# Two loads of 40 partitions cut into four, of 32 and of 8 partitions, in a kernel of mLSTM attention and two feed-forward layers

## Chip, cores, metric

One Trainium2 chip, one core. The metric is device time in microseconds of one launch, over several runs; smaller is better.

## What is computed

Three layers, one after the other, in float32.

1. An mLSTM attention over q, k, v of shape (2, 8, 768, 40): two batches, eight heads, 768 steps, 40 wide. For every step t and head:

```
m_new = max(f + m, i);  fs = exp(f + m - m_new);  is = exp(i - m_new)
C = fs * C + is * outer(v_t, k_t);   n = fs * n + is * k_t
y_t = sigmoid(o_t) * (C q_t) / max(|n . q_t|, 1)
```

2. A mixture of eight experts over the 1536 tokens (320 wide, 1024 inner). Noisy logits choose the best two experts of a token, softmax weights them, each expert is `relu(x w1) w2`.

3. A dense layer: `h = x w_in` (2048 wide), `g = h cos(h)`, result `g w_out`.

## The kernel before

**Attention.** The 768 steps of a batch are cut into NC = 6 pieces of 128 steps, so that there are 12 attention steps (`att_step(n)`, L858, n from 0 to 11, six for each batch). Within a piece the recurrence becomes matmuls: `mm_s` (L240) forms k times q for four pairs of heads, `mk_w` (L200) forms the decay weights by exponentials, `mk_p` (L251) multiplies both, `mm_out` (L300) multiplies by v and adds the part of the running state, `mm_state` and `mk_state` (L261, L281) carry the state on, `mk_q` (L233) scales q for the next piece, and `mk_y` (L316) divides and gates and stores the result `xt` in the DRAM tensor `xd`. All instructions are issued in an order written by hand: step n does the matmul `mm_s` for piece n+2, and its own `mm_out`, interleaved per pair of heads (L869 to L877).

**Loads.** All plain transfers are issued by SyncE (SP) in program order. `load_qk(n)` (L162) brings q and k of a piece into one of NB = 3 tiles `qk` of 128 partitions by 4 x 4 x 128 values. Even heads lie in partitions 0 to 39 and odd heads in 64 to 103; the other partitions stay zero from the start (L137, L138). A half is 40 rows of 3 x 4 x 128 values of 4 bytes, 6144 bytes each, contiguous in DRAM. `load_gb` (L171) reads the cumulated forget gates from the DRAM tensor `gd`, where `gates_a` (L85) has written them, and spreads them over all partitions; `load_kv` (L179) brings k and v by rows, `load_o` (L153) the output gates. `loads(n+1)` (L847) at the end of step n issues q and k of piece n+4, then `gb`, `kv` and, in the first steps, `ogt`. The tile `qk` that is filled again is the one that the multiplication of L238 (`qtt`, on POOL or DVE) has read for piece n+1. The store of `xt` (L330) follows on the same queue. Three pieces of q and k are loaded ahead of the first step (L817 to L822).

**Experts.** From step 6 on the router of batch 0 (`router_*`) runs between the steps, and weights of the first expert are loaded (`load_w`, L533, tile `wraw`). From step 9 on, expert steps (`expert_step`, L640) stand among the attention steps; each splits its weights into two float32r parts (L589, L591) and does three products in place of one (`mm1`, L594; `mm2`, L600). The dense layer follows in the same manner. This part, from about 95 us to the end, is most of the time.

Of the kernel before, what the change touches and what calls it, by code (L numbers as in the profile page):

```python
# [19 lines left out]
B, H, S, D = 2, 8, 768, 40  # L20
# [21 lines left out]
def tile_mlstm_moe_moe2(ctx, tc, qk, kv, og, gi, gf, wcat, noise, wm1, wm2, cst, out):  # L42
    nc = tc.nc
    V, A, G, T, Y = nc.vector, nc.scalar, nc.gpsimd, nc.tensor, nc.sync
# [89 lines left out]
    for i in range(NB):  # L134
        t = ap_.tile([128, 4, NH, C], FT, name=f"qk{i}")
# [4 lines left out]
    for i in range(2):  # L140
        t = ap_.tile([128, H, 64], FT, name=f"kb{i}")
        G.memset(t, 0.0)
        KBS.append(t)
    for i in range(2):
        t = ap_.tile([128, NH, 82], FT, name=f"st{i}")
# [16 lines left out]
    def load_qk(n):  # L162
        if n >= 2 * NC:
            return
        b, c = divmod(n, NC)
        d = L[n]
        t = d["qk"] = QKS[n % NB]
        Y.dma_start(t[0:D, 0:3], qk[b, c, 0])
        Y.dma_start(t[64:64 + D, 1:4], qk[b, c, 1])

    def load_gb(n):  # L171
        if n >= 2 * NC:
# [642 lines left out]

    Y.dma_start(ident, cst[:, 0:128])
    load_qk(0)  # L817
    load_kv(0)
    load_qk(1)
    load_o(0)  # L820
    load_kv(1)
    load_qk(2)  # L822
    gates_a(0, 1)
    gates_b(0, 1)
# [193 lines left out]
    for q in range(3):  # L1018
        for i in range(3):
            c = 3 * q + 3 + i  # L1020
# [25 lines left out]
    with tc.If(over > 0):  # L1046
        WD = [dr.tile([S, E], FT, name=f"wd{b}") for b in range(B)]
        for b in range(B):
            r = R[b]
# [6 lines left out]
        for b in range(B):  # L1056
            with tc.For_i(0, NC, 1) as it:
# [11 lines left out]
                for e in range(E):  # L1069
                    acc = psA()  # L1070
                    for f in range(8):
# [3 lines left out]
                        for k in range(3):  # L1075
                            r = slice(64 * (k == 2), 128)
# [20 lines left out]
                t = mp.tile([128, DM], FT, name="yt", tag="yt", bufs=3)  # L1097
# [76 lines left out]
```

## Time and profile before

| | us |
|---|---|
| median of three runs | 521.35 |
| the three runs | 517.87, 521.35, 522.74 |
| the profiled execution's own time | 519.47 |
| its span, first to last instruction | 517.8 |

The profiled execution's own time is its span and 1.67 us around it. Times in views are counted from the start of the span. PE is TensorE's matmul, PEld its weight load, DVE is VectorE, ACT ScalarE, POOL GpSimd, and a "q" behind an engine's name its queue.

### The profile page before, as it was taken

The page shows a single profiled execution, that of the slowest core. Times are in us where ns is not written, and L with a number is a line of the kernel's source. Part 1 is how long each engine was busy: PE and PEld are TensorE (multiplying, and loading weights), DVE is VectorE, ACT ScalarE, POOL GpSimd, SP SyncE. Part 2 cuts the span into 40 slices and gives each one's busy share as a digit, 9 for nine tenths or more (in the row PEclk, how much of TensorE's full clock was granted, in tenths as well). Part 3 has the DMA queues.
Part 4 walks back from the last instruction along what each step waited for, and adds up shares of the span by engine and source line. Part 5 has one row for each costly group of instructions (what it writes and reads, how often), then busy time and mean ns, then how long its engine had stood idle before and what let it go on. Part 6 is the DMA issues. An engine that isn't in the chain of part 4 may idle for free.

```text
span 517.8 us, 9017 instructions
## 1 busy us (share of the span) xinstructions
PE 489.4 (95%) x3198; PEld 469.2 (91%) x3198; DVE 368.6 (71%) x787; ACT 326.1 (63%) x695; POOL 274.6 (53%) x234
## 2 busy tenths in 40 slices
PE   4899989999999999999999997899999999999995
PEld 3798978899899999999999997899999999999994
DVE  8885595678468776778775678788855655787772
ACT  3658864566555554545454575578877777777772
POOL 6435456666856867595868686274355347300000
PEclk9999997999999999999999999999999999999999
DMA  6878883595472928290929193130021003001001
GB/s 182 252 264 276 271 276 120 174 331 204 172 287 87 338 67 319 85 379 22 367 92 315 58 362 118 42 104 14 1 70 47 1 1 103 13 2 38 2 1 44
DMA packets 25397, 76.37 MB, mean 147 GB/s; under 512 B 3872, under 2 KB 11392, under 8 KB 25344
## 3 DMA queue, kind: packets, MB, share of 16 engines
q1 hardware_dynamic: 22752, 67.11, 37.3%
q0 software_dynamic: 2592, 8.61, 5.4%
q8 instruction: 27, 0.44, 0.3%
q14 instruction: 26, 0.21, 0.1%
HBM read 66.47 MB, written 9.22 MB: 146 GB/s over the span
## 4 chain that ended last, share of the span: by engine, by line
PE 74%; DVE 12%; DMA 5%; ACT 5%; issue 3%; POOL 1%; SPq 0%; DVEq 0%; POOLq 0%; ACTq 0%
PE pS L598 35%; PE pA L607 11%; PE pA L604 10%; PE pA L603 10%; PE pM L559 2%; PE pA L616 1%; PE pA L615 1%; DMA gb<-gd 1%; DMA qk<-qk 1%; ACT wt L210 1%; DMA wraw<-wm 1%; PE pS L311 1%; DVE c_t L721 1%; DVE ogt L325 1%; DVE r_am L489 1%
## 5 line engine op out<-in xcount | busy, mean ns | idle before, releaser
L591 POOL TENSOR_TENSOR wl<-wraw,wh 128x704 fp32r<-128x704 f32 x69 | 122.9, 1790 | 61.0 <-ACT wh L589 53.5
L653 DVE SCALAR_TENSOR_TENSOR hb<-pS,hb 128x384 fp32r<-128x384 f32 (+2 forms) x128 | 45.9, 390 | 45.5 <-ACT hb L650 44.8
L589 ACT ACTIVATE wh<-wraw 128x704 fp32r<-128x704 f32 x80 | 62.9, 786 | 14.0 <-PE pA L615 9.1
L598 PE MATMUL pS<-xh,wh 128*128 128x448 f32 (+1 forms) x240 | 69.7, 344 | 0.7 <-ACT xh L561 0.5
L598 PE MATMUL pS<-xh,w 128*128 128x384 f32 x288 | 66.5, 340 | 1.6 <-DVE m_t L762 1.5
L598 PE MATMUL pS<-xh,wl 128*128 128x448 f32 (+1 forms) x240 | 65.7, 328 | 0.4 <-POOL wl L591 0.4
L604 PE MATMUL pA<-wl,hb 128*128 128x320 f32 x208 | 62.2, 308 | 0.0
L603 PE MATMUL pA<-wh,hb 128*128 128x320 f32 x208 | 62.0, 307 | 0.0
L747 ACT ACTIVATE m_t<-pS,magic 128x384 f32<-128x384 f32 x64 | 37.1, 580 | 27.9 <-PE pS L598 27.1
L650 ACT ACTIVATE hb<-pS 128x448 fp32r<-128x448 f32 (+1 forms) x80 | 37.7, 472 | 26.3 <-PE pS L598 19.3
L598 PEld LDWEIGHTS pS<-xh,w 128*128 128x128 f32 x288 | 49.8, 188 | 2.9 <-DVE m_t L762 2.9
L762 DVE SCALAR_TENSOR_TENSOR m_t<-m_t,pS 128x384 f32<-128x384 f32 x64 | 35.4, 553 | 16.8 <-ACT m_t L761 16.2
L607 PE MATMUL pA<-wh,hb 128*128 128x320 f32 x208 | 44.0, 310 | 2.8 <-DVE hb L653 2.7
L598 PEld LDWEIGHTS pS<-xh,wl 128*128 128x128 f32 x240 | 42.7, 188 | 2.9 <-POOL wl L591 0.5
L598 PEld LDWEIGHTS pS<-xh,wh 128*128 128x128 f32 x240 | 40.4, 189 | 2.0 <-ACT xh L561 0.6
L748 DVE TENSOR_SCALAR m_t<-m_t 128x384 f32<-128x384 f32 x64 | 23.1, 361 | 26.6 <-ACT m_t L747 26.4
L768 POOL TENSOR_TENSOR wl<-m_t,wh 128x384 fp32r<-128x384 f32 x25 | 25.5, 1018 | 30.3 <-ACT wh L766 21.2
L598 PE MATMUL pS<-xl,wh 128*128 128x448 f32 (+1 forms) x160 | 39.6, 328 | 0.1
L603 PEld LDWEIGHTS pA<-wh,hb 128*128 128x128 f32 x208 | 38.6, 186 | 0.8
L604 PEld LDWEIGHTS pA<-wl,hb 128*128 128x128 f32 x208 | 38.6, 186 | 0.6
L550 POOL DMA_INDIRECT xgt<-xd,idx x28 | 34.4, 1229 | 7.0 <-issue 2.5
L749 DVE SCALAR_TENSOR_TENSOR m_t<-pS,m_t 128x384 f32<-128x384 f32 x64 | 35.7, 558 | 2.2
(196 smaller groups left out, 1243.7 us busy)
## 6 DMA issues: line engine op xcount, KB each, us to landing
wraw<-wm SPq DMA_DIRECT2D x36, 704.0 KB
raw<-wm SPq DMA_DIRECT2D x16, 704.0 KB
qk<-qk SPq DMA_DIRECT2D x24, 240.0 KB
gb<-gd SPq DMA_DIRECT2D x10, 512.0 KB
kv<-kv SPq DMA_DIRECT2D x12, 324.0 KB
yd<-yt SPq DMA_DIRECT2D x22, 160.0 KB
wraw<-wm SPq DMA_DIRECT2D x8, 352.0 KB
ogt<-og SPq DMA_DIRECT2D x6, 320.0 KB
```

The source lines that it names most:

```text
L550: G.indirect_dma_start(out=t[:n, :], out_offset=None, in_=XD[0:S, :] if g < 2 else XD[:, :], in_offset=bass.IndirectOffsetOnAxis(ap=(idxe ...
L589: A.activation(wh, raw[:, f, :], AF.Copy)
L591: eng.tensor_tensor(out=wl, in0=raw[:, f, :], in1=wh.bitcast(FT), op=OP.subtract)
L598: T.matmul(p[:, :n], w[:, 128 * k:128 * k + 128], x[:, m, :], start=(i == 0), stop=(i == 7))
L603: T.matmul(a[:n, :DM], hh[:, s], wh[:, KW:], start=first, stop=False)
L604: T.matmul(a[:n, :DM], hh[:, s], wl[:, KW:], start=False, stop=False)
L607: T.matmul(a[:n, :DM], hl[:, s], wh[:, KW:], start=False, stop=last)
L650: A.activation(hh[:, :n], p[:, :n], AF.Relu)
L653: V.scalar_tensor_tensor(out=hb[:, o:o + z - a], in0=p[:, a:z], scalar=0.0, in1=hh[:, a:z].bitcast(FT), op0=OP.max, op1=OP.subtract)
L747: A.activation(t, m["p"], AF.Identity, bias=magic, scale=0.5 / PI)
L749: V.scalar_tensor_tensor(out=t, in0=m["p"], scalar=0.5 / PI, in1=t, op0=OP.mult, op1=OP.subtract)
L762: V.scalar_tensor_tensor(out=s, in0=s, scalar=1.0, in1=m["p"], op0=OP.subtract, op1=OP.mult)
```

## The change

The two loads of a `load_qk`, each of 40 partitions, become four: first partitions 0 to 31 of the even half, then of the odd half, then the remaining 8 partitions of each. Bytes, tiles, and the place in the program stay.

```
-        Y.dma_start(t[0:D, 0:3], qk[b, c, 0])
-        Y.dma_start(t[64:64 + D, 1:4], qk[b, c, 1])
+        for r in (slice(0, 32), slice(32, D)):
+            for s in range(2):
+                Y.dma_start(t[64 * s + r.start:64 * s + r.stop, s:s + 3], qk[b, c, s, r])
```

## Rows read from the trace of the kernel before

**Rows 1.** The page's span, and DMA's mean share in 40 equal slices.
```profile
span 517.8 us, 9017 instructions
...
DMA  6878883595472928290929193130021003001001
```
**Rows 2.** The page's chain that ended last: share of the span by engine, by line.
```profile
PE 74%; DVE 12%; DMA 5%; ACT 5%; issue 3%; POOL 1%; SPq 0%; DVEq 0%; POOLq 0%; ACTq 0%
PE pS L598 35%; PE pA L607 11%; PE pA L604 10%; PE pA L603 10%; PE pM L559 2%; PE pA L616 1%; PE pA L615 1%; DMA gb<-gd 1%; DMA qk<-qk 1%; ACT wt L210 1%; DMA wraw<-wm 1%; PE pS L311 1%; DVE c_t L721 1%; DVE ogt L325 1%; DVE r_am L489 1%
```
**Rows 3.** Attention stage: stretch, length, busy per engine (count), clock share, DMA share, GB/s.
```profile
16.00:76.00 60.00, 55.21 (x426) 51.07 (x424) 43.12 (x130) 42.58 (x127) 30.73 (x44) 1.00 0.88 279
```
**Rows 4.** Waits, 16 to 76 us: who for whom, us in total, times, longest.
```profile
ACT wt L210 <- DMA gb<-gd: 1.2, 1, 1.2
...
PE pA L248 <- DMA qk<-qk: 1.0, 2, 0.8
```
**Rows 5.** The chain in order of time, 27 to 49 us: start, us, what.
```profile
27.78 1.23 DVE g_all L97 x2
...
29.02 2.45 DMA gd<-g_all
...
31.54 6.00 DMA gb<-gd
...
37.62 1.29 ACT wt L210 x4
...
41.93 1.28 POOL qtt L238
...
43.59 5.95 DMA qk<-qk
```
**Rows 6.** Timeline of PE at three waits: start, us, ..., [idle before <-releaser].
```profile
23.56 0.45 PE L248 MATMUL pA<-qk 128*128 128x256 f32 x1 [0.81 <-DMA qk<-qk]
...
42.42 0.38 PE L356 MATMUL pM<-wc,xTt 128*128 128x128 f32 x1 [1.03 <-ACT xTt L349]
...
49.66 0.46 PE L248 MATMUL pA<-qk 128*128 128x256 f32 x1 [0.19 <-DMA qk<-qk]
```
**Rows 7.** Timeline of ACT, 36 to 38 us.
```profile
36.27 0.17 ACT L322 ACTIVATE den<-pS 128x8 f32<-128x8 f32 x1
37.62 0.69 ACT L210 ACTIVATE wt<-gb,tok 128x128 f32<-128x128 f32 x2 [1.17 <-DMA gb<-gd]
```
**Rows 8.** Timeline of DVE at 29.49 us.
```profile
29.49 0.17 DVE L323 TENSOR_SCALAR den<-den 128x8 f32<-128x8 f32 x1 [0.49 <-ACT den L322]
```
**Rows 9.** The page's DMA issues: the loads of q and k, KB each.
```profile
qk<-qk SPq DMA_DIRECT2D x24, 240.0 KB
```
**Rows 10.** Tile qk: the first of its two issues, ns min/median/max, first and last start.
```profile
L168 SPq DMA_DIRECT2D qk<-qk x12: 288/306/335, 2.6 to 67.4; - x12
```
**Rows 11.** Timeline of SP's queue, 29 to 32 us.
```profile
29.45 0.31 SPq L168 DMA_DIRECT2D qk<-qk  x1
...
30.64 0.42 SPq L155 DMA_DIRECT2D ogt<-og  x1
31.54 0.80 SPq L176 DMA_DIRECT2D gb<-gd  x2
```
**Rows 12.** Waits of SP's queue, 0 to 78 us.
```profile
SPq L168 <- POOL qtt L238: 14.6, 5, 4.4
...
SPq L330 <- DMA qk<-qk: 2.3, 2, 1.3
```
**Rows 13.** Rates in three short stretches (columns as in rows 3).
```profile
9.00:10.00 1.00, 1.00 (x5) 0.96 (x5) 0.93 (x4) 0.98 (x4) 0.00 (x0) 1.00 0.97 212
12.60:13.80 1.20, 1.08 (x3) 0.35 (x2) 1.13 (x4) 0.00 (x0) 0.15 (x1) 1.00 0.64 164
35.50:36.50 1.00, 0.94 (x11) 0.95 (x11) 0.36 (x3) 0.27 (x3) 0.00 (x0) 1.00 1.06 423
```
**Rows 14.** Line 248: instructions of PE's queue that only wait, ns min/median/max.
```profile
L248 PEldq EVENT_SEMAPHORE  x13: 51/51/1561, 7.9 to 76.6; - x13
```

## The prediction

> **What bounds the kernel now.** I read the page's chain first. TensorE's own work is 74% of it, nearly all in the expert and dense layers; DMA is 5%, and of that the loads of the changed line are 1% and the loads of the gates behind them on the same queue another 1% [rows 2]. So the change can act only through the first 78 us, where q and k are loaded; what is gained there reaches the end only if the later part shifts as a whole, which I assume, since its chain is PE's work.
>
> The windows say what kind of stage that is. From 16 to 76 us PE is busy 55.21 of 60 us, so all of PE's idle time there is 4.79 us, and DMA is at 0.88 of its share [rows 3], in slices with 7 to 9 tenths on the page [rows 1]: PE is the bound, and DMA stands close behind it. The waits tell what DMA costs now: ACT waited 1.2 us once for the gates, and PE 1.0 us in two waits for q and k [rows 4]. The timelines place them: PE at 23.56 (0.81) and 49.66 (0.19) [rows 6], ACT at 37.62 (1.17) [rows 7].
>
> The chain shows which of them counts. At 29.02 the gates go out to DRAM (2.45 us), at 31.54 they are read back, and that read takes 6.00 us. Then ACT's exponentials, POOL's `qtt` at 41.93, which frees a tile, and the load of q and k at 43.59, 5.95 us [rows 5], for which PE waits until 49.66 [rows 6]. Both transfers last that long because others stand before them: the `gd` transfer, with little in front, took 2.45 us.
>
> **The change part by part.** *The bytes.* A load of 240 KB stands 24 times on the page [rows 9]; a pair is 480 KB, 0.49 MB. What the new shape does to the rate no row shows. I bound it from both sides. In the stretch 12.6 to 13.8 only the last pair of the opening loads should be in flight, by the order of issue, and the rate is 164 GB/s; where a pair runs beside `kv` and `ogt` it is 212 in all; where gates, `kv` and `ogt` run it is 423 [rows 13]. 0.49 MB takes 3.0 us at 164, 2.3 us at 212 and 1.2 us at 423. So a pair now occupies the engines some 2.3 to 3.0 us, and at best 1.2: a gain of up to 1.8 us a pair. On the other side, two more transfers could each cost as much as a fixed part: if each row of the pair ran at the present lowest rate and each new transfer added its issue of 0.31 us [rows 10] in full, a pair would last 0.6 us longer; were the pieces of 8 as slow as `gd`'s lone 2.45 us, and only half of one hidden, 1.2 us longer. I take 0.6 us shorter, a fifth to a quarter of the present pair, nearer to the slow rows than to 423, since the destination partitions are the same as now.
>
> By the Trainium skill (DMA: Bandwidth & Descriptors, "Why a DMA increments its semaphore by 16 and not by 1") a transfer runs on the largest number of engines up to 16 that divides its outer dimension: 10 for 40 rows, 16 for 32, 8 for 8. The fullest engine would go from 8 rows of a pair to 6, an estimate of a quarter less. The rate of 164 against 423 agrees with a transfer that leaves engines idle, but doesn't prove it.
>
> *The gates' wait at 37.62.* Ahead of the gates in the queue stand one pair (from 29.45), `kv` and `ogt` [rows 11], and what was left of two earlier pairs. With 0.6 us less for each of three, the gates land up to 1.8 us earlier; 1.17 us suffices, so the whole wait goes even at 0.4 us a pair. What is late next is ACT's own order: `den` at 36.27 ends at 36.44 [rows 7]. Gain 1.17 us on the path; PE's wait of 1.03 at 42.42, which is for ACT [rows 6], is the same time further on, and is not counted again.
>
> *The waits for q and k.* That of 49.66 is on the path: 0.19 us more. That of 23.56 is not, since DVE's scans, from 27.78 to 29.01, set when the gates go out [rows 5]. Its 0.81 us lets PE run ahead, and then ACT's `den` is ready earlier: DVE's idle 0.49 us at 29.49 [rows 8] can go, and the `tok` copies behind it come earlier. I count half of it, 0.25 us.
>
> *SP's queue.* Two more issues a piece, 24 in all, of 0.31 us and some 0.06 between them: 0.37 each, 0.74 us later for `gb`, `kv`, `ogt` and the `xd` store behind them. At the path's place, the gates of 31.54: `ogt`'s issue would end at 31.06 + 0.74 = 31.80, so the gates are issued 0.3 us later [rows 11]. The cover is the queue of transfers before them: 6.00 against 2.45 us, 3.5 us of queueing [rows 5]. If that cover went, it would cost 0.3 us. SP itself waits 14.6 us for `qtt` [rows 12], so it has time. SP also waits for earlier landings: before the `xd` store 2.3 us in two waits for pairs [rows 12]; I read that as a limited number of transfers on the way, of which a pair now takes four places. With a full queue in front this delays no byte; I put it at nothing, and at 0.4 us an issue without the cover.
>
> *Waits in PE.* `mm_s` now has four landings to wait for. Line 248 has 13 instructions that only wait, median 51 ns [rows 14]; one more for each of 12 pieces is 0.6 us, most of it while earlier matmuls run. I take 0.1 us; the bounds are 0 and 0.6. POOL and DVE read the same tile; they have idle time there (30.73 and 43.12 busy of 60) [rows 3].
>
> *Sum.* 1.17 + 0.19 + 0.25 - 0.1 = 1.5 us. The profiled execution has a span of 517.8 us [rows 1] and a time of 519.47: 516.3 and 518.0. It lies 1.9 us under the median of 521.35, so against the median I forecast 519.9 us.
>
> **The rivals.** *No faster transfer* (nothing gained). The new pieces run no faster: 32 partitions are the same ones that 40 filled, and the even and the odd half still follow each other. For it: the pair's rate is low with whatever runs beside it, 212 with other loads and 164 without [rows 13], which a limit at the destination would also give. Against it: nothing in the rows. A pair remains at 2.3 to 3.0 us, and the time at 521.35, plus the 0.1 us of waits: 521.4. The Trainium skill (SBUF — State Buffer, "Door 1: The DMA port swizzle") would have it so: 32 partitions of one half reach 8 of 16 ports, about 217 GB/s of 435 as an estimate, 2.3 us for the pair before and after. The 212 GB/s agrees with that; the 164 is under it.
>
> *The loads become the bound* (slower). A pair gets longer by d, because pieces of 8 rows hold up the queue. The place is the queue of transfers between 16 and 76 us, with nine pairs (of pieces 3 to 11). Its idle share is 0.12 of 60 us [rows 3], 7.2 us, or 0.8 us a pair: beyond that every further microsecond of d costs nine. Below it, the two loads that PE already waits for, and the gates' 1.17 us wait, each pass d on; two of these are in the chain [rows 5]. At d = 1.2 us: 2 x 1.2 + 9 x 0.4 = 6.0 us, 527.4 us. It decides from about d = 1.0. For it: DMA's 0.88. Against it: even the slowest bound without a fixed part is 0.6, which costs 1.2 us and stays near the median.
>
> *More than the waits* (faster). With a queue that is far emptier, all of PE's idle time in the stage could go: 4.79 us [rows 3], 516.6. Against it: most of the other waits are for ACT, DVE and the router, not for DMA, whose waits come to 2.2 us [rows 4].
>
> **How the numbers follow.** A measurement of this kernel tells about 1%, 5.2 us, from no change. Forecast (1 to 2.5 us less): 0.58. No faster transfer: 0.24. Loads the bound: 0.10. More than the waits: 0.08, half of it over 5.2 us. So faster by over 1%: 0.04, slower by over 1%: 0.10, within 1%: 0.86. The three runs lie 4.9 us apart, so a median may be off by 2 us or so: 516.5 to 524.0 us holds the forecast, the first rival and part of the last, and leaves out the slow one and half of the last, 0.14, and a little for the spread.
>
> **What would show it.** Right: the wait of ACT for `gb` and those of PE for `qk` are gone or under 0.2 us; the chain's gates read shrinks from 6.00 us to under 5, and at its end stands PE or DVE; rates above 212 in the opening stretch; 48 issues of `qk` of 0.3 us. Wrong: the waits stay at 1.2 and 1.0 us (no faster transfer), or PE's wait for `qk` grows in several steps and the DMA share of 16 to 76 us exceeds 0.95 (slower).

## The result, and the profile after

The median of 22 runs is 524.3 us (519.68 to 529.54), that of 22 runs of the kernel before 521.25. Three runs of the changed kernel lie over 1.5% above its fastest and are left out of the ratio, which is 1.0057, 95% interval 1.0033 to 1.0081. So the change costs some 3 us. The forecast was 1.5 us the other way; the time lies within 1% of the kernel before, and just over the upper end of the range, 524.0. The profiled execution took 523.83 us, its span is 522.1, against 519.47 and 517.8.

The page of the changed kernel, its span, DMA slices, first queue and the head of its chain (of the kernel before, the queue's line read 22752 packets, 67.11 MB, 37.3%):

```profile
span 522.1 us, 9063 instructions
...
DMA  7799996667273927391847375030011003001001
...
q1 hardware_dynamic: 23088, 67.11, 39.0%
...
PE 74%; DVE 10%; DMA 8%; issue 3%; POOL 2%; ACT 2%; SPq 0%; POOLq 0%; DVEq 0%; ACTq 0%
```

The same bytes now take 39.0% of the engines' span in place of 37.3%, and DMA holds 8% of the chain in place of 5% [rows 2].

The windows of 0 to 16 us before the change, then of 0 to 16 and 16 to 76 us after it: stretch, length, busy per engine (count), clock share, DMA share, GB/s; the last answers to [rows 3]:

```profile
0.00:16.00 16.00, 7.83 (x30) 5.85 (x31) 13.41 (x36) 5.44 (x17) 8.40 (x14) 1.00 0.62 174
```

```profile
0.00:16.00 16.00, 7.78 (x30) 5.87 (x31) 13.38 (x36) 5.45 (x17) 8.39 (x14) 1.00 0.81 165
16.00:76.00 60.00, 53.29 (x399) 49.24 (x398) 37.68 (x116) 40.36 (x120) 28.17 (x42) 0.97 0.92 256
```

The DMA engines are busier, 0.81 against 0.62 and then 0.92 against 0.88, and move less, 165 GB/s against 174 and 256 against 279. PE has 399 matmuls in the 60 us in place of 426. The stage is behind; a part of that is the clock, as shown below.

Tile `xt` on DVE, the last instruction of an attention step and of the combining of the experts (ns min/median/max, first and last start in us), first before the change, then after it:

```profile
L328 DVE SCALAR_TENSOR_TENSOR xt<-pS,ogt x12: 491/492/493, 21.8 to 104.9; 128x320 f32<-128x320 f32 x12
L683 DVE SCALAR_TENSOR_TENSOR xt<-yg,r_w x12: 540/552/2995, 313.1 to 456.4; 128x320 f32<-128x320 f32 x12
```

```profile
L329 DVE SCALAR_TENSOR_TENSOR xt<-pS,ogt x12: 491/492/492, 21.8 to 109.7; 128x320 f32<-128x320 f32 x12
L684 DVE SCALAR_TENSOR_TENSOR xt<-yg,r_w x12: 540/552/3001, 317.6 to 461.0; 128x320 f32<-128x320 f32 x12
```

The last attention step is 4.8 us late, the last of the experts 4.6: the loss is there when the attention steps end, and is only carried on.

What stands out first in this execution is the way of the gates. The chain of the changed kernel from 14 us on (start, us, what):

```profile
14.12 4.91 DMA gd<-g_all
...
19.05 4.17 DMA gb<-gd
```

ACT's timeline at this place, before the change and after it:

```profile
20.68 2.44 ACT L210 ACTIVATE wt<-gb,tok 128x128 f32<-128x128 f32 x8
```

```profile
23.30 0.98 ACT L211 ACTIVATE wt<-gb,tok 128x128 f32<-128x128 f32 x3 [2.52 <-DMA gb<-gd]
```

The gates go out at 14.1 us in both kernels (SP's issue stands at 14.14 before, at 14.12 after). Before, the read of `gb` was issued at 15.99, so `gd` had landed after some 1.8 us, and ACT went on without a wait; now the small `gd` transfer takes 4.91 us, the read is issued at 19.05, and ACT starts 2.6 us later. Some 1.7 us follow at PE, as its windows show, before and after:

```profile
27.00:30.40 3.40, 3.40 (x31) 3.30 (x29) 2.75 (x7) 1.66 (x7) 0.93 (x2) 1.00 0.53 170
```

```profile
23.00:27.00 4.00, 0.69 (x4) 0.67 (x5) 1.70 (x4) 3.59 (x10) 1.27 (x2) 1.00 1.00 273
27.00:30.40 3.40, 3.40 (x15) 3.22 (x15) 3.26 (x8) 0.00 (x0) 0.87 (x1) 0.50 1.08 261
```

PE was busy 0.69 of 4 us, and then ran 3.4 us at a granted clock of 0.50, the 1.2 GHz level, with 15 matmuls in the time of 31. Half of 3.4 us is 1.7; with the 2.6 us this makes 4.3, and the second `xt` is 4.4 us late (30.52 us before, 34.92 after). This is also the difference of the spans, but that is chance, for it doesn't stay. The last two `xt` of the attention, before and after:

```profile
98.77 0.49 DVE L328 SCALAR_TENSOR_TENSOR xt<-pS,ogt 128x320 f32<-128x320 f32 x1
...
104.93 0.49 DVE L328 SCALAR_TENSOR_TENSOR xt<-pS,ogt 128x320 f32<-128x320 f32 x1
```

```profile
99.09 0.49 DVE L329 SCALAR_TENSOR_TENSOR xt<-pS,ogt 128x320 f32<-128x320 f32 x1
...
109.73 0.49 DVE L329 SCALAR_TENSOR_TENSOR xt<-pS,ogt 128x320 f32<-128x320 f32 x1
```

At the eleventh `xt` the changed kernel is 0.3 us behind, and the last step then takes it 10.6 us in place of 6.2. The kernel before has its own stretch at the low clock, later and twice as long; the changed kernel has a second one in its last step, behind a wait of PE for POOL (the window before, then the wait and the window after):

```profile
78.40:85.10 6.70, 6.70 (x30) 6.34 (x30) 4.20 (x13) 0.87 (x2) 4.16 (x6) 0.50 0.61 200
```

```profile
100.57 0.45 PE L308 MATMUL pS<-st,qtt 128*128 128x82 f32 x2 [1.74 <-POOL qtt L239]
```

```profile
102.10:105.50 3.40, 3.40 (x19) 3.40 (x17) 1.59 (x5) 1.17 (x2) 0.04 (x1) 0.50 0.95 206
```

So both executions spend about the same time at the low clock in this stage, 6.7 and 2 x 3.4 us, and the clock explains none of the 4.8 us between these two. POOL was late there after it had stood 3.0 us for a gather of the experts (`xgt`, until 91.77), which is no load of q and k; whether that gather was late because of the change was not traced. Net of the low stretches, each counted at half its length, the changed kernel is an estimated 2.7 us behind at the second `xt`, 2.0 at the eleventh and 4.8 at the twelfth. One execution of each kernel doesn't tell where the 3 us of the medians are made, so the runs below go by their ratios.

Over many runs the clock does have a share. Each run's mean granted clock is on record, and (1 - clock) x span estimates what the low level cost it, if PE had work throughout. That is 4.9 us on average over the 129 runs of the kernel before that stand beside the experiments, and 6.1 us over the 19 runs of the change in the ratio; the mean spans are 519.2 and 522.2. So by this estimate some 1.2 of the 3.0 us came as lower clock, and 1.8 us are there without it.

The waits of the changed kernel, 16 to 76 us, as in [rows 4]:

```profile
ACT wt L211 <- DMA gb<-gd: 3.0, 2, 2.5
...
PE pA L249 <- DMA qk<-qk: 1.2, 1, 1.2
```

And those of SP's queue, 0 to 78 us, as in [rows 12]:

```profile
SPq L170 <- POOL qtt L239: 6.1, 3, 2.3
SPq L170 <- DMA qk<-qk: 5.8, 11, 1.5
SPq L177 <- DMA gd<-g_all: 2.9, 2, 2.5
...
SPq L155 <- DMA ogt<-og: 2.4, 2, 1.3
SPq L186 <- DMA kv<-kv: 2.4, 2, 1.3
```

SP now waits for landings before nearly every kind of load: all such lines of this view sum to 23.5 us, to 7.4 before the change. (Line 177 reads what `gd` wrote; the other loads' data don't depend on what they wait for.) The trace's semaphores say why: SP's transfers signal on eight of them in turn, and each is issued only when the one eight places before it has landed. A pair takes four of the eight places now.

### The profile page after: what moved, and what is told of

Read it like the earlier page. It is cut to its first block, busy times and chain, and to the rows that moved or that the text cites. A ratio compares the mean times of both kernels' runs of the same rounds, so it can differ in the third digit from the quotient of the medians.

```text
span 522.1 us, 9063 instructions
## 1 busy us (share of the span) xinstructions
PE 489.8 (94%) x3198; PEld 469.4 (90%) x3198; DVE 368.1 (70%) x787; ACT 326.0 (62%) x695; POOL 273.7 (52%) x234
## 3 DMA queue, kind: packets, MB, share of 16 engines
q1 hardware_dynamic: 23088, 67.11, 39.0%
## 4 chain that ended last, share of the span: by engine, by line
PE 74%; DVE 10%; DMA 8%; issue 3%; POOL 2%; ACT 2%; SPq 0%; POOLq 0%; DVEq 0%; ACTq 0%
PE pS L599 35%; PE pA L608 10%; PE pA L605 10%; PE pA L604 10%; DMA qk<-qk 4%; PE pM L560 2%; PE pA L617 1%; PE pA L616 1%; PE pS L312 1%; DMA xgt<-xd,idxe 1%; DMA gd<-g_all 1%; PE pA L249 1%; DVE c_t L722 1%; DMA gb<-gd 1%; POOL qtt L239 1%
## 5 line engine op out<-in xcount | busy, mean ns | idle before, releaser
L769 POOL TENSOR_TENSOR wl<-m_t,wh 128x384 fp32r<-128x384 f32 x25 | 25.4, 1017 | 30.4 <-ACT wh L767 21.2
```

## The experiments

Ratios are to the kernel before, run on the same chip, with 95% intervals. Edits not shown are named in the text.

**The shapes by themselves.** A kernel without the computation, which loads six pairs in each of seven shapes, one shape after the other.

```
for s in range(2):                       # 40
    Y.dma_start(t[64*s:64*s + 40, s:s + 3], qk[b, c, s])
for r in (slice(0, 32), slice(32, 40)):  # 32 and 8
    for s in range(2):
        Y.dma_start(t[64*s + r.start:64*s + r.stop, s:s + 3], qk[b, c, s, r])
```

> This kernel leaves the whole computation out: SyncE loads six tiles of q and k in one shape, waits for all of them, and goes on to the next shape: pairs of 40; 32+8; 20+20; 32 alone; 32 rows on every fourth partition; 8 alone; the pair's bytes over 128 partitions. Theory A (where the rows land): pieces of 32 partitions of one half of the tile put more transfer engines on the same write paths, so their bytes go slower, and the number of transfers counts for little. Then 20+20 lasts as long as pairs of 40 within 10%, 32+8 at least 20% longer, and 32 rows on every fourth partition go at least 1.5 times as fast as 32 neighbouring ones. Theory B (number): every transfer costs a fixed time, some 0.5 us, or four transfers of a pair fill the places that SyncE has on the way. Then 20+20 is as slow as 32+8, both longer than pairs of 40 by about 1 us a pair, and spreading the rows changes nothing.

Windows inside five of the shapes (stretch, length, DVE and POOL busy, clock, DMA share, GB/s): 40 partitions, and its second half alone; 32 and 8; 20 and 20; 32 neighbouring ones alone; 32 on every fourth partition alone.

```profile
9.00:21.00 12.00, 4.28 (x3) 0.00 (x0) 1.00 0.65 225
15.00:21.00 6.00, 0.00 (x0) 0.00 (x0) 1.00 0.65 255
25.00:38.00 13.00, 0.00 (x0) 0.00 (x0) 1.00 0.85 209
42.00:54.00 12.00, 0.00 (x0) 0.00 (x0) 1.00 0.63 222
58.00:66.00 8.00, 0.00 (x0) 0.00 (x0) 1.00 0.99 260
70.00:78.00 8.00, 0.00 (x0) 0.00 (x0) 1.00 0.86 276
```

The new shape is no faster: 209 against 225 GB/s, and the 225 are low, since SyncE waited 1.8 us in that row for DVE, which was still clearing the tiles; behind that, from 15 to 21 us, 40 partitions ran at 255. The new shape keeps more of the engines busy, 0.85 against 0.65. 32 partitions keep 0.99 busy and reach 260, hardly more than 40 with 0.65; spreading them gives 276. So it is not a lack of engines that holds 40 partitions at 255 GB/s, and neither is it mainly which partitions they are. From first issue to first issue of the next row, six pairs took 16.3 us with 40 (14.5 without the 1.8), 17.3 with 32 and 8 and 16.1 with 20 and 20. That is some 0.3 to 0.5 us a pair for four loads in place of two, under theory B's 1 us, and spreading gave far less than theory A's half more. Neither theory is met.

**Twenty and twenty.** `slice(0, 20), slice(20, D)` in place of the change's slices.

> The kernel with each load cut into 20 and 20 partitions: as many transfers as 32 and 8. Theory A: as the kernel before within 0.3%. Theory B: as the kernel with 32 and 8, 0.4 to 0.8% slower than before.

525.28 us against 521.39, ratio 1.0055 [1.003, 1.008], as theory B said: as slow as the change, though 20 and 20 keep no more engines busy than 40 does (0.63 and 0.65 above). The shares 32 and 8 don't matter; four loads in place of two do.

**Fewer bytes.** Only the two loads of 32 partitions; 8 of 40 rows of q and k are left out.

> The kernel loads rows 0 to 31 of each half alone, one transfer a half; 8 of 40 rows of q and k stay zero, so a fifth of the bytes is left out. Theory A: pieces of 32 are slow by themselves, so with a fifth less to load it is still no faster than before (0 to 0.4% slower). Theory B: two transfers a pair and fewer bytes, 0.2 to 0.5% faster than before.

519.58 us, ratio 0.9971 [0.9936, 1.0006]. A fifth of these bytes less, in two loads a pair, is worth 0.3%, as theory B said; the interval reaches from 0.64% down to nothing. Not much was to be had from faster pairs.

**Another order of the four.** The loops over `s` and `r` exchanged, so that both pieces of the even half come first.

> As the change (32 and 8), but both pieces of the even half before those of the odd half. Theory A: the piece of 8 of one half can run beside the piece of 32 of the other, so it may be a little faster than the change; 0.2 to 0.7% slower than before. Theory B: the number is the same, so the same as the change, 0.4 to 0.8% slower than before.

528.15 us in four runs, ratio 1.0099 [1.0067, 1.0131]: by the middle 0.4% worse than the change, with the same pieces, and above what either theory said; the two intervals overlap a little. Why the order should matter stays open.

**The opening by itself.** A kernel with only the loads of the start, in their order (pair, `kv`, pair, `ogt`, `kv`, pair), in several shapes, and three pairs alone.

```
opening(a40); opening(a32_8); opening(a20_20); opening(a40_tiny); opening(a32)
opening(none); pairs(a40); pairs(a32_8)
```

> This kernel leaves the whole computation out: SyncE issues the opening's loads of the kernel (three pairs of q and k, with kv, ogt and kv between them) in one shape of the pairs after another, each time after all has landed: 40; 32+8; 20+20; 40 with two transfers of 64 bytes behind each pair; 32 alone; no pairs; then three pairs alone, 40 and 32+8; and the first four again. Theory P (places): the transfers that can be on the way are limited in number, and what counts is how many a pair takes. Then 40 with tiny transfers takes as long as 20+20, and both at least 1 us longer than 40. Theory S (small pieces): the pieces of 8 rows, which crowd on few partitions, are slow beside other transfers. Then tiny transfers change nothing (within 0.4 us), 20+20 lies within 1 us of 40, and 32+8 is at least 2 us longer than 40, although three pairs alone differ by under 0.7 us.

The timeline of SP's queue: the first issue of a block, and the store that waits for its last pair; opening with 40, opening with 32 and 8, three pairs alone with 40 and with 32 and 8.

```profile
7.13 0.71 SPq L66 DMA_DIRECT2D qk<-qk  x2
...
19.47 0.37 SPq L60 DMA_DIRECT2D out<-qk  x1
...
20.83 1.59 SPq L66 DMA_DIRECT2D qk<-qk  x4
...
35.56 0.37 SPq L60 DMA_DIRECT2D out<-qk  x1
...
85.19 2.49 SPq L66 DMA_DIRECT2D qk<-qk  x6
...
96.12 0.37 SPq L60 DMA_DIRECT2D out<-qk  x1
...
97.48 5.12 SPq L66 DMA_DIRECT2D qk<-qk  x12
...
106.76 0.37 SPq L60 DMA_DIRECT2D out<-qk  x1
```

Alone, three pairs take 10.93 us with 40 and 9.28 with 32 and 8, 0.55 us less a pair, measured once. Among `kv` and `ogt` it turns round: 12.34 against 14.73 us (12.78 against 15.44 in a repetition), 0.8 to 0.9 us more a pair. 20 and 20 took 14.62 and 14.88; two loads of 64 bytes behind each pair, which move nothing to speak of, 13.73 and 13.49. So more transfers cost something by themselves, 1.05 us on average, and data in more pieces twice as much: each theory is right in part.

**One part at a time, in the kernel.** First only pairs 3 to 11 split, then only pairs 0 to 2; then pairs 0 to 2 whole, with two loads of 64 bytes behind each.

```
for r in (slice(0, 32), slice(32, D)) if n >= 3 else (slice(0, D),):   # late
for r in (slice(0, 32), slice(32, D)) if n < 3 else (slice(0, D),):    # opening
...
if n < 3:                                                              # tiny
    for i in range(2):
        tiny = ap_.tile([1, 16], FT, name=f"tiny{n}{i}")
        Y.dma_start(tiny, cst[0:1, 0:16])
```

> Pairs 0 to 2 (the opening) as before, pairs 3 to 11 cut into 32 and 8. Theory O (opening): the loss arises in the first 20 us alone, where the gates' way through DRAM lands behind the three pairs and SyncE holds back all that follows. Then this is within 0.3% of before. Theory E (everywhere): each pair lasts longer, and nine of twelve make three quarters of the loss: 0.3 to 0.6% slower than before.

> Pairs 0 to 2 cut into 32 and 8, pairs 3 to 11 as before. Theory O: the whole loss, 0.4 to 0.9% slower than before, and the first gates land after 22 us in place of 20. Theory E: a quarter of the loss, under 0.25% slower.

> The kernel before, with two extra loads of 64 bytes behind each of pairs 0 to 2: as many transfers in the opening as the change has, without smaller pieces. Theory P (places): the third pair is issued late and ends late, 0.3% slower or more. Theory S (small pieces): within 0.15% of before.

Late pairs 1.0060 [1.0035, 1.0084], opening 1.0028 [1.0002, 1.0055], tiny loads in the opening 1.0002 [0.9974, 1.0031]. Both parts of the change cost, the late pairs alone as much as all of it, so theory O falls; that the two don't add up lies within the intervals. It also means that the long wait for the gates at 23 us isn't needed for the loss: with the late pairs alone split, ACT starts there at 20.67, as in the kernel before. The tiny loads in the opening cost nothing that shows, as theory S said, though they had cost 1.05 us in the opening by itself.

**A chain of steps by itself.** Five times a pair, 512 KB, `kv` and a store of 160 KB, without the computation, each shape twice.

```
def steps(load):
    for n in range(N):
        load(n)
        rest(n)
```

> This kernel leaves the whole computation out: SyncE issues five steps of the kernel's loads and stores (a pair of q and k; 512 KB as the gates are; kv; a store of 160 KB to DRAM), waits for no engine, and then takes the next shape of the pair: 40; 32+8; 20+20; 40 with two transfers of 64 bytes; 32+8 with the pieces of 8 on POOL's queue; no pair; pairs alone of 40 and of 32+8; the first five again. Theory P (places): the number of transfers on the way is limited, so that 32+8, 20+20 and 40 with tiny ones all take at least 3 us longer for the five steps than 40, and the pieces of 8 on POOL's queue bring 32+8 back to 40 within 1.5 us. Theory M (mixing): what costs is that a pair of small pieces spreads over engines that would else carry the other transfers: 32+8 is at least 3 us longer than 40 wherever its pieces of 8 are issued, while the tiny transfers cost under 1.5 us; pairs alone in 32+8 are no longer than in 40.

The timeline of SP's queue, the first issue of a block and the store behind its last pair, in the second pass: 40, then 32 and 8. Behind them a wait of SP's queue in the first pass.

```profile
216.96 0.74 SPq L70 DMA_DIRECT2D qk<-qk  x2
...
244.23 0.34 SPq L64 DMA_DIRECT2D out<-qk  x1
...
246.73 1.59 SPq L70 DMA_DIRECT2D qk<-qk  x4
...
279.31 0.34 SPq L64 DMA_DIRECT2D out<-qk  x1
```

```profile
SPq L96 <- DVE kv L60: 5.8, 1, 5.8
```

In the first and the second pass 32 and 8 took 30.4 and 32.6 us, 20 and 20 31.6 and 31.2, 40 and two tiny ones 31.9 and 35.1; with the 8s on POOL's queue 26.9 and 25.4. 40 partitions took 30.8 and 27.3; the first pass of it holds 5.8 us in which SyncE waited for DVE to clear a tile of `kv`, so the second is the one to compare with. More transfers on SP's queue are 3.9 to 7.8 us slower in that pass, even when they bring next to nothing, and the same pieces are fast when half of them leave that queue: theory P here. Five pairs alone took 12.6 us with 40 and 13.5 with 32 and 8 in this kernel, so the gain of three pairs alone didn't come again.

**That in the kernel.** Two tiny loads behind each of the 12 pairs of 40; and the change with its loads of 8 on POOL's queue (`G.dma_start`).

> The kernel before, with two extra loads of 64 bytes behind each of the twelve pairs: the number of transfers of the change, without smaller pieces. Theory P (places): as slow as the change, 0.3 to 0.8% slower than before. Theory M (mixing): within 0.2% of before.

> The change with the pieces of 8 partitions issued by POOL, so that SyncE has two transfers a pair as before. Theory P (places): under 0.25% slower than before, if POOL has time for 24 issues of about 1 us. Theory M (mixing): as the change or slower, 0.4% or more.

Tiny loads: 522.72 us, 1.0027 [1.0004, 1.0051], about half of the change's loss with no piece cut, between what the two theories said; the interval reaches from nearly none of the loss to most of it. The 8s on POOL: 526.07, 1.0125 [1.0082, 1.0168], worse than on SP. There POOL's issue takes a median of 538 ns and stands in order behind POOL's multiplications, and the waits of 16 to 76 us read:

```profile
POOL kb L231 <- DMA kv<-kv: 4.0, 2, 3.6
...
PE pA L249 <- DMA qk<-qk: 3.5, 3, 1.2
```

What the chain of steps gained in a kernel without computation is not to be had here.

**Giving places back.** The 18 loads of `kv` and `ogt`, which are wanted later, move to POOL's queue: with 40 partitions, with 32 and 8, and only the six of `ogt` with 40.

```
-        Y.dma_start(t, og[:, 2 * i:2 * i + 2, :])
+        G.dma_start(t, og[:, 2 * i:2 * i + 2, :])
-        Y.dma_start(t, kv[b, c])
+        G.dma_start(t, kv[b, c])
```

> The kernel before (40 partitions, two loads a pair) with the 18 loads of kv and ogt issued by POOL in place of SP. Theory P (SP's transfers take a limited number of places in turn, and each new one waits for the landing of the one eight before it): the pair, gb and xd store keep the places to themselves, SP's waits for landings in 0 to 78 us fall from some 7 us to under 4, and the time is 0.1 to 0.5% under the kernel before. Rival M (pieces of different size that run side by side slow each other down, whatever the number of places): kv and ogt now run beside the pairs still more, 0 to 0.3% slower. Rival I (POOL's issues come late behind its multiplications): PE or ACT waits for kv or ogt, 0.5% or more slower.

> The change (32 and 8 partitions, four loads a pair) with the 18 loads of kv and ogt issued by POOL. Theory P: SP has 18 transfers fewer for its places, its waits for landings fall from 23.5 us to some 15 us, and the loss against the kernel before falls from 0.57% to 0.2% or less. Rival M: the loss stays at 0.4 to 0.8%. Rival I: 1% or more slower, as much behind the same kernel with 40 partitions as the change is behind the kernel before.

> The kernel before with only the 6 loads of ogt issued by POOL. Theory P: 0 to 0.2% under the kernel before, SP's waits for landings in 0 to 78 us at 5 to 7 us. Rival M: the same time, within 0.1%. Rival I: POOL's issue comes late for tanh, ACT waits, 0.2% or more slower.

With 40: 0.9995 [0.9971, 1.0019]; with 32 and 8: 1.0065 [1.003, 1.01]; `ogt` alone: 0.9984 [0.9955, 1.0012]. The largest wait of SP's queue with 32 and 8, 0 to 78 us, and its largest for a landing, and the windows of 16 to 76 us, with 40 and with 32 and 8:

```profile
SPq L170 <- POOL qtt L239: 13.0, 5, 3.4
...
SPq L170 <- DMA gb<-gd: 4.7, 3, 2.3
```

```profile
16.00:76.00 60.00, 54.34 (x421) 50.41 (x420) 40.16 (x122) 41.20 (x120) 38.43 (x58) 1.00 0.88 262
```

```profile
16.00:76.00 60.00, 51.37 (x384) 47.16 (x383) 35.41 (x105) 38.06 (x113) 35.43 (x54) 0.97 0.96 248
```

SP's waits for landings sum to 13.5 us in place of 23.5, as theory P said (2.6 with 40), and the loss stayed, as rival M said. With 40 the interval holds no change, so it doesn't decide between them. The engines are busy 0.96 and move 248 GB/s. So the places are not the whole.

**Engines or pieces?** The same two lines moved, with 20 and 20, and with 40 and two tiny loads.

> Pairs as four loads of 20 partitions, kv and ogt issued by POOL. Theory E (two costs: four loads a pair use up the places of SP's transfers, and 32 partitions keep more transfer engines busy for the same bytes than 20 or 40 do, which takes them from the other loads): with the places given back and 20 partitions, which in the load test kept as few engines busy as 40, the loss against the kernel before falls from 0.55% to 0 to 0.3%; DMA share in 16 to 76 us about 0.88, where 32 and 8 had 0.96. Rival N (it is the number of loads a pair alone, the pieces' shape does not matter): as slow as the same kernel with 32 and 8, 0.5 to 0.8%.

> Pairs as two loads of 40 partitions and two of 64 bytes, kv and ogt issued by POOL. Theory E: the 64-byte loads cost places alone, and these are given back: the loss falls from 0.27% to 0 to 0.15%. Rival N: it stays at 0.3% or grows to 0.5 to 0.8%, as with 32 and 8.

20 and 20: 1.0052 [1.0022, 1.0082]; tiny: 1.0017 [0.9993, 1.004]. Windows of 20 and 20:

```profile
16.00:76.00 60.00, 53.56 (x379) 49.55 (x378) 35.46 (x105) 37.62 (x111) 34.56 (x54) 0.91 0.84 237
```

Theory E falls on 20 and 20: at a DMA share of 0.84, without the busy engines of 32 and 8, the pair in four pieces loses about as much. The two kernels were run beside each other, and 20 and 20 took 2.1 us more on average (523.6 against 521.5), so data in four pieces cost more than data in two and two tiny loads. With the tiny loads alone the interval holds both theories.

**Whom do they make late?** The pair of each step issued behind `gb`, `kv` and `ogt` in place of ahead of them.

```
     def loads(n):
-        load_qk(n + 3)
...
+        load_qk(n + 3)
```

> The kernel before (two loads of 40 partitions a pair) with the pair of each step issued last, behind gb, kv and ogt. Theory B (gb and kv stand behind the pair and come late): gb no longer waits for POOL's qtt and for the pair, ACT's 1.2 us wait for gb goes, 0 to 0.4% under the kernel before. Rival Q (the pair itself is what comes late): PE's waits for qk in 16 to 76 us grow from 1.0 to 3 us or more, 0.2 to 0.6% slower.

> The change (32 and 8 partitions, four loads a pair) with the pair of each step issued last, behind gb, kv and ogt. Theory B: the pieces have only the next step's loads and the store behind them, and the distance to the same order with 40 partitions falls from 0.57% to 0.2% or less. Rival Q: PE waits for the pieces, and the distance stays at 0.4% or more. A part of it stays under both, from the three pairs ahead of the first step (0.28% when these alone were split).

With 40: 529.88 us, 1.0177 [1.0135, 1.0219]; with 32 and 8: 531.29, 1.0216 [1.0173, 1.0259]. Rival Q holds for the first: with 40 partitions PE now waits for the pair, 16 to 76 us:

```profile
PE pA L248 <- DMA qk<-qk: 7.9, 2, 4.3
```

So the pair has no slack to give; it is needed soon after the tile is free. The loss is three times what rival Q said; by the estimate from the mean clocks 9.0 us of these runs is low clock, in place of 4.9. The distance of the two kernels, 1.0216 / 1.0177 = 1.004, doesn't tell the theories apart, since the intervals overlap.

No version beat the kernel before by more than the uncertainty.

## Why the prediction was wrong

**The bound.** Right in that the difference stands when the attention steps end and is carried on unchanged (4.8 us there, 4.6 at the end of the experts). That the waits for q and k and for the gates make all of it is not shown: in the profiled execution a wait for POOL in the last step has a part, and over the runs the clock.

**The pair's duration: the step that failed.** "I take 0.6 us shorter" was the first term from which the gain of 1.17 + 0.19 + 0.25 us came. For pairs alone it held once, 0.55 us in the run of the opening, and not in the longer rows of pairs, 209 against 255 GB/s for six and 13.5 against 12.6 us for five. Among other loads, in the opening's order without the computation, a pair got 0.8 to 0.9 us longer. The rows that I took for the pair's own rate, 164 to 212 GB/s [rows 13], were of mixed stretches: alone, pairs of 40 ran at 255, so that a pair takes an estimated 1.9 us and not 2.3 to 3.0, and there was less to gain. The other side, 0.6 to 1.2 us longer, stood in the prediction, and I took the wrong one. By the Trainium skill (DMA: Bandwidth & Descriptors, "Why a DMA increments its semaphore by 16 and not by 1") the engines used would go from 10 to 16 and 8. The trace agrees: DMA shares of 0.65, near 10 of 16, and 0.99; and 23088 - 22752 = 336 packets more, 24 x (16 + 8 - 10). My estimate of a quarter less time from it doesn't hold: rates were 255 GB/s with 40 and 260 with 32, and 209 with the 8s.

**SP's queue: the second part.** "With a full queue in front this delays no byte; I put it at nothing." I had seen the limit on transfers under way and that a pair would take four places. But SP's waits for landings went from 7.4 to 23.5 us, and two loads of 64 bytes a pair cost 0.27%, 1.4 us of the 3, or 0.06 us for each of the 24 loads more. The issues themselves came as forecast, 48 of a median of 326 ns. The queue in front was not always full: between 16 and 24 us the DMA share fell to 0.67, where it had been 0.89.

**The gates' wait.** It didn't go. It grew from 1.2 to 3.0 us, and moved to an earlier place, 23.3 us, where the kernel before had none. I had put the small `gd` transfer at 2.45 us, as in a quiet stretch; behind twelve pieces it took 4.91, where it had taken some 1.8 at the same place, and the reads of `gb` had to wait for it. The loss doesn't hang on this wait, as the run with only the late pairs split shows.

**The waits for q and k, and in PE.** That of 23.56 went over into a wait for the gates; the term of 0.25 us was not to be seen by itself. The instructions that only wait came as counted, 25 at the line of `mm_s` in place of 13, with a median of 51 ns; whether 0.1 us of them is on the path no run shows. PE's clock stood in no term; by the estimate above it is 1.2 us of the 3.

**The rivals.** *No faster transfer* was nearest for the pair alone, and too low on the time by 3 us. By the Trainium skill (SBUF — State Buffer, "Door 1: The DMA port swizzle") the neighbouring partitions would have been the limit, at an estimated 217 GB/s; 32 neighbouring ones ran at 260 and 32 spread ones at 276, so here they cost 6%. These loads went to both halves in turn, and no run loads one half alone. *The loads become the bound* had the right sign, and a d of 0.8 us was met in the opening by itself; its marks were not: the DMA share of 16 to 76 us is 0.92 and not over 0.95, PE waited 1.2 us once for q and k, and the waits that grew were ACT's and POOL's. Its 6 us were twice the loss. It had 0.10, and what I held against it was misread: the 0.6 us "without a fixed part" were nothing but a fixed part, two issues of 0.31. *More than the waits* had half of its chance over 5.2 us, beyond its own price of 4.79.

**What stays open.** That four loads with data in place of two cost the 3 us is shown; why is shown in part. Places may explain up to half: tiny loads cost 0.27%, and with the places given back 0.17% with an interval that holds zero. The rest, 0.5% for data in four pieces with the places given back, is explained neither by engines held nor by partitions, and why mixed loads are slower than the sum of their parts was not found.

## What to carry to other kernels

A load's rate measured alone says little of what it does among others: here the same pieces gained 0.55 us a pair or lost 0.2 alone, and lost 0.8 in the mix. Before a transfer is cut, count how many transfers the queue may have under way and what small one that others wait for stands behind the pieces (`gd` went from some 1.8 to 4.91 us); sum the queue's waits for landings that have nothing to do with their data. And where two profiles differ by a few us, compare them step by step and look for the stretches at the low clock in both, before a wait that is seen in one of them is called the loss.

## What was not expected of the hardware

- A rate of 255 GB/s with 0.65 of the engines busy, 222 with 0.63, 209 with 0.85 and 260 with 0.99: more busy engines moved hardly more.
- Two loads of 64 bytes behind each of three pairs cost 1.05 us of a 12.56 us opening sequence without computation, and 0.02% (interval -0.26 to 0.31) in the kernel; behind all twelve pairs they cost 0.27%.
- The order of the four pieces alone may be worth 0.4%, by four runs.
